# Causal masks written by VectorE, one conversion tile cleared once, and a new fixed order

## The chip, the cores and the metric

One core of a Trainium2 chip. The time is that of one execution on the device, in microseconds; the kernel before has a median of 922.75 us in three runs (922.51 to 926.28). Engines: PE (TensorE: matmuls, into PSUM), DVE (VectorE), ACT (ScalarE), POOL (GpSimd), SP (SyncE, which only issues DMAs).

## The reference

q, k and v are float32 of shape (4, 8, 576, 64): 4 batches, 8 heads, 576 positions. A causal mask in blocks of 64 positions, a softmax, the product with v; the heads are put together to 2304 tokens of 512 features. Two feed-forward layers follow, each 512 to 2048 to 512.

```python
scores = scale * np.matmul(q, k.transpose(0, 1, 3, 2))
mask = block_i >= block_j                  # blocks of 64 positions
scores = np.where(mask, scores, -1000000000.0)
attn = softmax(scores)                     # maximum subtracted, sum + 1e-9
x = concat_heads(np.matmul(attn, v))       # (2304, 512)
h = x @ w_in1;  x = (h * np.tanh(softplus(h))) @ w_out1
h = np.maximum(x @ w_in2, 0.0);  out = (h * h) @ w_out2
```

## The kernel before, in words

**Tokens and passes.** The 2304 tokens are six chunks of 384. Chunks 0 and 1 hold the first 192 positions of the batches ("low" tiles), chunks 2 to 5 the other 384 positions ("high" tiles). A pass is one layer on one chunk: sixteen column blocks f; for each, a first product into `hp` (twelve float16 matmuls of 384 columns, L1206), an activation on ACT (L1212), a split of its result into two float16 parts (ACT, DVE or POOL, L1034 to L1036, and DVE, L744), and a second product into four accumulators `acc` (twelve matmuls, L1272). The first pass (layer 0, chunk 0) runs in float32 instead (L1226, L1231, L1241).

**Attention.** One attention unit is two heads of one batch. A low unit (`attention_lo`) computes its scores by float32 matmuls (L967), row maxima on DVE (L972, L973), the maxima times minus the scale (L974, DVE, SBUF to SBUF), exponentials on ACT (L977), sums and reciprocals on DVE (L980, L982), the scaling of the tiles (ACT L749 or DVE L751), transposes on PE (L990 to L993), a copy (L720 or L722), and the product with v (L1005, L1006). Eight low units of chunk 0 come first, since the first pass needs their result `xs`. A high unit (`attention_hi`) has three score groups of six matmuls (`scores`, L833; 320, 128 and 448 columns, and one more of 448 that needs no mask), then maxima (L843), exponentials (L851), probabilities in two float16 parts (L870, L744), transposes by DMA, and the product with v (L931).

**The mask.** The last 64 key columns of a group are forbidden to the upper 64 query rows. PE adds to them: `above` (ones in its first 64 columns) times `never` (minus 1e24), one matmul for each head (L836) behind the group's six; in a low unit one matmul of 128 columns (L968). Sixteen low units have one, sixteen high units three pairs.

**Weights.** Each weight unit (a megabyte, `decode`) is loaded as raw words (L1053), and a float32 tile is put together from two pieces: POOL clears the tile (L1058), ACT or DVE converts the upper halves into it (the rebias, L1060 or L1061), and DVE shifts the lower bits and ORs them in, in place (the combine, L1062). Layer 0 has sixteen units, each with a tile of its own (parts of `first`, `late` and `ws`); layer 1 has sixteen that share three tiles `wf`. Sums of squares (L1074) and a split into float16 parts follow.

**What sets the order.** The program is a list of 4491 tasks with an engine each. A compressed string, `PLAN`, holds the order of all of them, and the engine of each task that could run on more than one (`planned`). Each engine executes its own tasks in that order and waits at semaphores. The costs given with the tasks and `Sched.opened` serve the search that once made the string; with a string there they change nothing. Tiles of one ring (`R[...]`) are used in turn, and a task waits for the last users of its buffer. `spare["ab"]` is the pair of PSUM banks that all high units share.

Of the kernel before, what the change touches and what calls it, by code (L numbers as in the profile page):

```python
# [59 lines left out]
def seg_len(tiles):  # L60
# [30 lines left out]
    "c-p<02iR4`)wZA6=ST+uAt0hC#b5^uDk7kWD9r*Wh*UuZL2M|ZkzzqbDRyiSMPh=8B?5|K7b&8E(yR2|+Y4vbfA97}Os+rX`>rq7;q0^b>@_p1&GW3qJKUKa"  # L91
    "t?)a>9kil4#T};ucDg=t<u$^cqO2~|POIT|SR-w>?N-)pv*K!j%w}uj_Sr`3pgp$UcH0IU>DF3lRhGA{R#RJSzvWqB9jDG(X!YD4TZ7bU3$#<e+FV;{&aGgr"
    "<F(O#K(?^<*;-p*CEadYW%KM;bDD!x9p|l>R@y9UuJu+(g^(+&pG~fm=Cj(5I#EkmXN&cAhioAl71C))errdmjCR{+`pI@$NlmdIZJRB(GgK7WMK;wk`UZ_Y"
    "v`^XRD>UC`Uz)cS_L*(6ndn|b<u%>@tTk3ZbJ1x8*PMNUmyETR*l2BFuSMv*7~8V=VU-P5sPzt{R@gFRwy@Fxdkd)zwiiDwuyuTP+SAC)Mt+;UjJLL8-7@=&"
    "O-K9tG!5Agxm#mhbtj%a+jZ6*MBy==>Dp@v(l@Fbzc=95%~(84*YR1;>MeDz*0SzwyIogd&n&x63y{m%ExHyRe&+XE{P=)=;rb;}_`>R_DIWTaPa}P5pV|!T"
    "u20Zpwq2=-_Mp0Gw=U6lcxVScJYQc~d!484MBo#m`MGV@?K+v6r)#oR(KUL{s%w>&=p){BP!;u7Ro;w8i&J%`PEi|8vR-=I%BvM4Z`mwOWlj~1w-fcX#@TCp"
    "#@gq2;Y7V+BW#R)rE(h03eVUZcB=|&6u%?+JZ;nTx(z0C8WNG0?Q)Gk>Y)AA>T0wO+OyV5AL~sstF7VIOmA2{;=NT*G4dL@{DeKDK<o69J!(TVOb_G1Yw`1N"
    "yMP=UY7dfq9jq^rc+&bHz17ONXY`oeZGF&uJ=c|1%uUl`yNw;rCr`doA8TX3*nQT;YN(UVCjy`7NBahUPt-njw>kEA{XqPBX$Eh)*fn;&-qEqvgX>&tV&xdW"
    "1^;za8?xprS5nLLwJk-<Z_T^Qu)Yad+SIN@_r^BSE+pQKY^WA!tb5-Y*i*VvAKL?(t*3OcjkCAy2|Ym;g&sd&-SJ07eArhf@ca-tQjz#n)Q5QQOlI~`S-pTC"
    "Khzj9t~2vS+gR6v+3%=_dg?_h$om(pmhN>A+s)+qaO;mXrSuTzYJ_gq4DGj5_&#f$bgvC@gKU6R)(|~nZ@D(?`X^#`9n#mk3VPBWu!g!zFS-U=VP(|Q8Z)OZ"  # L100
    "T0F$HnJxo+ZnF*ev=iRFTr;gJ8P$c;c7u9x5>L~`dQ)|fX`x&3#I+i%Zni=_>=yeYS$4ASwkdX&KC`c_E#FggBRN@JpIZwn@9Jn4C$6QP<SroJk9TiaW9zA_"
    "@oiD;YJ!b7U~OrgqoZ`Wovjk&d2vnvej@j-vI6dMJkSb+Y-}G{Rn@mjD(9ZH%gC~eK#!{6S|ioAlfcxqc8*=hsjrBq-T)KoXuWEYGexoVOpxac^6P9nNA=05"
    "3%Fly!$6jEts2>UHt2T{oZDwaj#Uc~!77ZL#A;3*t)v}qd#sclvUcESo|WcX){0qE@TfSR>R|<~h&3bMZ?z1bX%6l^u2C9920y0Pu&zC5yU7M{;`+18RIWdf"
    "y)Tg^Ly61tdK$bK72!%PGOaRqcj^&*Jq3(@p6t1sTzix(ooEk(>|e0zW9p}J_PEB{Kv1VI(*3}pLgd*P*AL`)n#_8N43qBHaI~3bgRtmneQ%HIkbi@_nbuDu"
    "ZJ&Qg53$d8_NE5vIla!)cy{PQPETR|r@-4@>^+7oAFlh|?fSc|@Q-lc6`dFP3E<Z|Amkj*`$?e8mC-8w(D@$SX`?{8ndHq|@X2=`D~QNsPRC%RALN{W=3lkW"
    "`jgt}eQdgi`2%#5TDhU%S0C`9r|u*3o&d3XlKXw_N!_XnWO`#_{JcG)$MN_vWNK-!x+hq9vTjg6B66#H&Ta;q?jVx~Sre=ZXI(|^4gzJ)RTFiEUz+P4aOpM;"
    "09hM=#O*krO<|(CoQuBJ%Ia}KPK1e@AeZB$Gz04|hY7obGfi}<&bNl_KhG}Xlx*XSbO5t{BJ*yr_MGr8WWi<NdVAH<N;04Z*>tw9hEdVP8nA9FID9s`S63Cg"
    "S{K2yGsxlFh*cfcgPR)aHFCWMd~l&12mUrf>X1G|zN9WB7eCVkES^L5ovgE2v4pnTBvs}7O|$z|ll`jW`%5?x@4`f<V)rRl*^bv6c;f&uD@m50t_oI(yg3Wx"
    "D9yWqb_s|*7DTSDqO5QXnQ;)bE<tqvY)6sx#gN=ZwDLf-N0^_rET{8*6*dRY--&MCU!cukp;?~yeAjVuc5=RUlXv@VmoEyJHPd!q3ic_Wtvt`S_CC<_w#(N0"
    "@o4d`wZW&-O>U*_17RC!s<m}**&^SZ{C`kiz)&q+F=A0bvwcC%OIEY|`5<RUcOEFe24))%_Yb9l%ENcdt-cG{zph(?rWbQvXeF3E5)>=W?ls&TYKCjnfZxm9"  # L110
# [90 lines left out]
class Sched:  # L201
# [76 lines left out]
    def opened(self, t, name):  # L278

        others = [o for o in ("PE", "ACT", "DVE") if o != name]  # L280
        return max((self.shut[b, o] + self.SEM[o][name] for b in t.banks for o in others if (b, o) in self.shut), default=0.0)
# [274 lines left out]
def c_mm16(n):  # L556
    return 2.5 + n / 2.4
# [1038 lines left out]
```

## Time and profile before

| | |
|---|---|
| median of 3 runs | 922.75 us |
| the profiled execution | 925.42 us |
| its span, first to last instruction | 923.6 us |
| PE busy | 895.7 us (97%) |
| DVE busy | 575.5 us (62%) |
| ACT busy | 575.1 us (62%) |
| POOL busy | 63.6 us (7%) |
| mean granted clock of PE | 0.992 |

Busy time is the time in which at least one instruction of the engine is under way. The span is what the trace shows; the execution's own time has a little around it. A wait of PE costs time as long as PE is the engine that ends last; idle time elsewhere need not.

### The profile page before, as it was taken

The numbers are of one execution on the slowest core, as the hardware profiler recorded it, in microseconds if no ns is written. First come the engines' busy times: TensorE is split into PE (matmuls) and PEld (weight loads), VectorE is DVE, ScalarE is ACT, GpSimd is POOL, SyncE is SP. The second block draws the span as 40 slices with busy tenths as digits, with TensorE's granted clock in tenths as the row PEclk, the third lists the DMA queues.
The fourth block names the chain that finished last, engine by engine and source line by source line (L and its number), as shares of the span: only waits on it lengthen the run. The fifth ranks groups of instructions, "written<-read, shape, count | busy, mean of one in ns | idle before, by whom it ended". The sixth has DMA issues, their size and how long they took to land. (4 is left out here: it accounts for less than half of the span.)

```text
span 923.6 us, 15581 instructions
## 1 busy us (share of the span) xinstructions
PE 895.7 (97%) x5786; PEld 533.2 (58%) x5786; DVE 575.5 (62%) x1432; ACT 575.1 (62%) x1121; POOL 63.6 (7%) x86
## 2 busy tenths in 40 slices
PE   4999999999999999999999999999999999999997
PEld 4666555555555555555566555555666666666664
DVE  6668999999989877586721686976531341331211
ACT  3988899999977655447322786987642333544442
POOL 6000201121211100010000000000000000000000
PEclk8899999999999999999999999999999999999999
DMA  7597556999688899738732388696732222343530
GB/s 272 205 362 288 176 159 156 310 291 290 248 299 198 263 231 234 223 107 199 245 98 83 108 224 211 180 241 160 161 101 70 69 69 69 115 137 137 171 114 35
DMA packets 141772, 168.79 MB, mean 183 GB/s; under 512 B 105856, under 2 KB 110976, under 8 KB 141696
## 3 DMA queue, kind: packets, MB, share of 16 engines
q1 hardware_dynamic: 141696, 167.79, 61.2%
q8 instruction: 45, 0.74, 0.3%
q14 instruction: 31, 0.25, 0.1%
HBM read 125.30 MB, written 17.30 MB: 154 GB/s over the span
## 5 line engine op out<-in xcount | busy, mean ns | idle before, releaser
L744 DVE SCALAR_TENSOR_TENSOR g<-h,cst,g 128x384 f16<-128x384 f32 x176 | 108.7, 619 | 222.4 <-ACT g L1034 218.1
L1212 ACT ACTIVATE h<-hp,cst 128x384 f32<-128x384 f32 x176 | 101.3, 577 | 216.9 <-PE hp L1206 205.7
L1272 PE MATMUL acc<-g,ws 128*128 128x384 f16 x1128 | 228.2, 326 | 0.0
L1272 PE MATMUL acc<-g,raw 128*128 128x384 f16 x984 | 205.2, 326 | 1.6 <-ACT ev L1285 1.6
L1206 PE MATMUL hp<-x,first 128*128 128x384 f16 x768 | 154.8, 326 | 1.0 <-ACT h L1212 0.9
L1272 PEld LDWEIGHTS <-ws 128*128 128x128 f16 x1128 | 108.7, 98 | 72.8 <-issue 2.2
L1272 PEld LDWEIGHTS <-raw 128*128 128x128 f16 x984 | 95.3, 98 | 65.5 <-issue 3.3
L1206 PEld LDWEIGHTS <-first 128*128 128x128 f16 x960 | 92.4, 98 | 63.8 <-issue 3.9
L1206 PE MATMUL hp<-x,raw 128*128 128x384 f16 x552 | 117.9, 326 | 0.0
L1034 ACT ACTIVATE g<-h,cst 128x384 f16<-128x384 f32 x119 | 72.8, 613 | 27.8 <-PE acc L1272 25.6
L1206 PEld LDWEIGHTS <-raw 128*128 128x128 f16 x648 | 61.6, 98 | 40.8 <-issue 1.9
L1206 PE MATMUL hp<-x,ws 128*128 128x384 f16 x408 | 84.7, 326 | 0.4 <-DMA ws<-wspill 0.4
L744 DVE SCALAR_TENSOR_TENSOR pb<-pad,st,pb 128x384 f16<-128x384 f32 (+2 forms) x96 | 71.1, 750 | 13.9 <-ACT pb L870 13.9
L870 ACT ACTIVATE pb<-pad,st 128x384 f16<-128x384 f32 (+2 forms) x96 | 66.4, 713 | 21.3 <-DVE st L863 6.4
L851 ACT ACTIVATE pad<-spare,st,sq 128x448 f32<-128x448 f32 (+1 forms) x96 | 65.1, 680 | 9.8 <-DVE st L846 4.7
L1206 PEld LDWEIGHTS <-ws 128*128 128x128 f16 x504 | 47.8, 98 | 30.8 <-DMA ws<-wspill 0.5
L843 DVE TENSOR_REDUCE st<-spare 128x2 f32<-128x896 f32 (+1 forms) x48 | 47.8, 996 | 10.3 <-PE spare L836 7.6
L1226 PE MATMUL hp<-xs,first 128*128 128x384 f32 x128 | 47.5, 491 | 0.0
L1206 PE MATMUL hp<-late,first 128*128 128x384 f16 x192 | 41.5, 326 | 0.0
L833 PE MATMUL spare<-q 64*128 64x448 f16 (+2 forms) x384 | 38.5, 306 | 1.5 <-ACT pad L851 1.1
L1217 ACT ACTIVATE h<-h 128x384 f32<-128x384 f32 x75 | 38.4, 514 | 0.6
L1241 PE MATMUL acc<-h,late 128*128 128x384 f32 x96 | 36.9, 495 | 0.2 <-ACT h L1231 0.2
(238 smaller groups left out, 1122.9 us busy)
## 6 DMA issues: line engine op xcount, KB each, us to landing
ws<-wspill SPq DMA_DIRECT2D x68, 512.0 KB, 4.6
raw<-wspill SPq DMA_DIRECT2D x68, 512.0 KB, 4.1
raw<-in_w_dram SPq DMA_DIRECT2D x27, 1023.8 KB, 6.5
wspill<-wn SPq DMA_DIRECT2D x24, 512.0 KB, 3.9
qk<-in_qp_dram SPq DMA_DIRECT2D x16, 480.0 KB, 4.6
vs<-in_va_dram SPq DMA_DIRECT2D x16, 320.0 KB, 4.1
pad<-in_w_dram SPq DMA_DIRECT2D x5, 1023.8 KB, 6.8
out_dram<-ev SPq DMA_DIRECT2D x24, 192.0 KB, 2.4
```

What stands on the lines that cost most here:

```text
L744: return sch.add("DVE", c_dve(n) + 62 * ap, lambda: nc.vector.scalar_tensor_tensor(dst(), a(), s() if ap else s, c(), op0, op1), r=r, w=w, ...
L833: nc.tensor.matmul(out=pp.t[:, hd, o:o + k1 - k0], lhsT=qh.t[rows, u, a:a + 128], rhs=qh.t[rows, w, nq + k0:nq + k1], start=p == 0, stop=p ...
L843: sch.add("DVE", c_dve(2 * (o1 - o0)), lambda: nc.vector.reduce_max(both(st, j, r0), pp.t[r0:, :, o0:o1], axis=AX.X), w=[(pp, 0), (st, j)])
L851: t = sch.add("ACT", c_act(o1 - o0, True, 3), lambda hd=hd: nc.scalar.activation(pf[hd].t[r0:, k0:k0 + o1 - o0], pp.t[r0:, hd, o0:o1], AF. ...
L870: sch.add("ACT", c_act(n, False, 1), lambda pb=pb, pv=pv, s=s: nc.scalar.activation(pb.t[:, 0:i + 1, 0, :], pv(), AF.Copy, scale=s()), r=[ ...
L1034: "ACT": ("ACT", c_act(n, False, 1), lambda: nc.scalar.activation(dst(0), src(), AF.Copy, scale=s()), False),
L1206: nc.tensor.matmul(out=hp.t[:, 0:n], lhsT=w.t[:, f % 2, a, 128 * k:128 * k + 128], rhs=x.t[:, c, k, 0:n], start=k == 0 and i == 0, stop=k ...
L1212: sch.add("ACT", c_act(n, True, 1), lambda: nc.scalar.activation(h.t[:, 0:n], hp.t[:, 0:n], (AF.Mish, AF.Relu)[l], scale=hs()), r=[(cst, ( ...
L1217: "ACT": ("ACT", c_act(n), lambda: nc.scalar.activation(hv(), hv(), AF.Square), False),
L1226: nc.tensor.matmul(out=hp.t[:, 0:n], lhsT=wf.t[:, 512 * (f % 2) + 128 * k:512 * (f % 2) + 128 * k + 128], rhs=xs.t[:, k, 0:n], start=k == ...
L1241: ts.append(sch.add("PE", c_mm(4 * n), lambda m=m, acc=acc: nc.tensor.matmul(out=acc.t[:, 0:n], lhsT=wf.t[:, 512 * (f % 2) + 128 * m:512 * ...
L1272: nc.tensor.matmul(out=acc.t[:, 0:n], lhsT=wo.t[:, f % 2, a, 128 * m:128 * m + 128], rhs=g.t[:, c, 0:n], start=f == 0 and i == 0, stop=f = ...
```

## The change

Four things. The mask matmuls are gone, and DVE writes a large negative number into the forbidden part of the scores, in PSUM, between the matmuls and the row maximum. For layer 0 the rebias goes into one separate tile `top`, cleared once in the prologue, whose low halves stay zero; the combine reads it and writes the weight tile, so the sixteen clears on POOL are dropped. Layer 1 is as before. The ring `us` has eight buffers instead of six. The order string is new; costs and `opened` are those with which it was searched.

```diff
-    R["us"] = sb("us", [128, 2 * NGRP], F32, 6)
+    R["us"] = sb("us", [128, 2 * NGRP], F32, 8)
...
+    top = pad.bitcast(F32)[:, 2048:3072]
+    R["top"] = fixed([top])
...
     make_identity(nc, ident)
+    nc.gpsimd.memset(top, 0.0)
...
-    above = cp.tile([128, 128], BF16, name="above")
-    nc.vector.memset(above[:, 0:64], 1.0)
-    nc.vector.memset(above[:, 64:128], 0.0)
-    never = cp.tile([128, 2], BF16, name="never")
-    nc.vector.memset(never, -1e24)
...
-            for i in R["raw"].insts:
+            for i in R["raw"].insts + R["top"].insts:
...
-                                         start=p == 0, stop=p == 2 and not mask)
-                for hd in range(2 if mask else 0):
-                    nc.tensor.matmul(out=pp.t[:, hd, o + k1 - k0 - 64:o + k1 - k0], lhsT=above, rhs=never[:, 0:1].to_broadcast([128, 64]), start=False, stop=True)
+                                         start=p == 0, stop=p == 2)
...
+            sch.add("DVE", 110.0, lambda pp=pp, n=n: nc.vector.memset(pp.t[0:64, :, n - 64:n], -1e25), w=[(pp, 0)])
             peak(st, 0, pp, 0, 0, n)
             if i == 2:
+                sch.add("DVE", 110.0, lambda pp=pp, n=n: nc.vector.memset(pp.t[0:64, :, n + 64:n + 128], -1e25), w=[(pp, 0)])
                 sch.add("DVE", c_dve(256), lambda pp=pp, n=n: nc.vector.tensor_copy(tail.t, pp.t[:, :, n:n + 128]), w=[(pp, 0), tail])
...
-                nc.tensor.matmul(out=pp.t[:, o:o + m], lhsT=qs.t[:, q:q + 128], rhs=qs.t[:, k:k + m], start=o == 0, stop=False)
-            nc.tensor.matmul(out=pp.t[:, 128:256], lhsT=above, rhs=never[:, 0:1].to_broadcast([128, 128]), start=False, stop=True)
+                nc.tensor.matmul(out=pp.t[:, o:o + m], lhsT=qs.t[:, q:q + 128], rhs=qs.t[:, k:k + m], start=True, stop=True)
...
+        sch.add("DVE", 135.0, lambda: nc.vector.memset(pp.t[0:64, 128:256], -1e9 / scale), w=[pp])
...
-        high = lambda: wf.t.bitcast(F16).rearrange("p (c two) -> p c two", two=2)[:, :, 1]
-        sch.add("POOL", 1000.0, lambda: nc.gpsimd.memset(wf.t, 0.0), w=[wf])
+        top = wf if l else R["top"].new()
+        high = lambda: top.t.bitcast(F16).rearrange("p (c two) -> p c two", two=2)[:, :, 1]
+        if l:
+            sch.add("POOL", 1000.0, lambda: nc.gpsimd.memset(wf.t, 0.0), w=[wf])
...
-            U(wf.t), mids(), 13, U(wf.t), ALU.logical_shift_right, ALU.bitwise_or), r=[raw], w=[wf], lock=True)
+            U(wf.t), mids(), 13, U(top.t), ALU.logical_shift_right, ALU.bitwise_or), r=[raw, top], w=[wf], lock=True)
```

The order strings can be decoded: three bytes a task, two for its number and one for its engine. Before: PE 1738 tasks, DVE 1426, ACT 871, POOL 80, SP 376. After: PE 1738, DVE 1523, ACT 848, POOL 54, SP 376. Ahead of the first matmul of the first pass stand 57 ACT, 76 DVE and 19 POOL tasks before, and 49, 95 and 7 after.

## Rows read from the trace of the kernel before

**Rows 1.** The page's busy table: engine, busy us, share, instructions.
```profile
span 923.6 us, 15581 instructions
PE 895.7 (97%) x5786; PEld 533.2 (58%) x5786; DVE 575.5 (62%) x1432; ACT 575.1 (62%) x1121; POOL 63.6 (7%) x86
```
**Rows 2.** Busy time by stretch: length, then each engine's busy us and instructions.
```profile
core 0: us, PE busy (x) PEld busy (x) DVE busy (x) ACT busy (x) POOL busy (x), PEclk, DMA share, GB/s
0.00:23.00 23.00, 10.80 (x52) 10.22 (x54) 14.15 (x34) 7.01 (x26) 14.44 (x25) 0.83 0.75 274
23.00:46.00 23.00, 21.93 (x134) 15.91 (x135) 15.99 (x55) 21.14 (x68) 0.00 (x0) 0.87 0.58 203
23.00:92.00 69.00, 67.66 (x325) 44.67 (x326) 50.75 (x142) 60.36 (x152) 0.64 (x2) 0.96 0.76 284
92.00:277.00 185.00, 181.01 (x1133) 103.03 (x1132) 175.32 (x425) 171.47 (x278) 31.57 (x39) 1.00 0.79 241
139.00:462.00 323.00, 314.21 (x2197) 182.58 (x2196) 274.39 (x693) 232.40 (x418) 37.79 (x47) 1.00 0.83 235
```
**Rows 3.** PE's waits: who, for whom, us in total, times, longest.
```profile
PE acc L990 <- ACT pt L749: 8.2, 1, 8.2
PE acc L967 <- DMA qk<-in_qk_dram: 4.0, 1, 4.0
...
PE acc L1272 <- ACT ev L1285: 1.6, 1, 1.6
```
**Rows 4.** Order of time at the start: start, us, what; idle before it in brackets.
```profile
2.10 0.23 POOL L962 MEMSET pt<- 128x64 f32 x2
2.26 1.84 POOL L1058 MEMSET late<- 128x1024 f32 x2
...
6.80 8.22 DVE L974 TENSOR_SCALAR st<-st 128x3 f32<-128x3 f32 x1
...
14.05 0.95 POOL L1058 MEMSET first<- 128x1024 f32 x1
15.12 0.42 ACT L977 ACTIVATE pt<-acc,st 128x192 f32<-128x192 f32 x1 [13.11 <-DVE st L973]
...
19.35 0.45 PE L990 MATMUL acc<-ident,pt 128*128 128x128 f32 x1 [8.23 <-ACT pt L749]
```
**Rows 5.** Order of time on PE: two score groups, and the first pass's first matmuls.
```profile
9.98 1.08 PE L967 MATMUL hp<-vs 128*128 128x192 f32 x6
...
20.23 1.81 PE L967 MATMUL acc<-vs 128*128 128x192 f32 x6
...
41.72 1.51 PE L1226 MATMUL hp<-xs,first 128*128 128x384 f32 x4
```
**Rows 6.** Groups by line and shape: count, busy us, mean ns of one, idle before.
```profile
L973 DVE TENSOR_REDUCE st<-spare 128x1 f32<-128x64 f32 x8 | 1.7, 216 | 0.0
L889 DVE COPY tl<-spare 128x256 f32<-128x256 f32 x16 | 7.3, 458 | 0.0
L749 ACT ACTIVATE pt<-pt,st 128x192 f32<-128x192 f32 x14 | 6.4, 456 | 0.3 <-DVE st L982 0.3
L720 ACT ACTIVATE pt<-spare 128x448 f32<-128x448 f32 x5 | 2.7, 535 | 0.1
L1074 ACT ACTIVATE wsq<-first 128x1024 bf16<-128x1024 f32 x8 | 8.4, 1055 | 0.1
```
**Rows 7.** The same view: rebias on ACT and combine on DVE.
```profile
L1060 ACT ACTIVATE first<-raw 128x1024 f16<-128x1024 bf16 x2 | 2.7, 1352 | 0.0
L1062 DVE SCALAR_TENSOR_TENSOR late<-raw,late 128x1024 uint32<-128x1024 uint32 x4 | 4.8, 1212 | 2.6 <-ACT late L1060 2.6
```
**Rows 8.** PE around masked and unmasked scores; all mask matmuls; those of 92:277.
```profile
580.56 0.74 PE L833 MATMUL spare<-q 64*128 64x448 f16 x6
581.23 0.23 PE L836 MATMUL spare<-never,above 128*128 128x64 bf16 x2
581.31 0.65 PE L1206 MATMUL hp<-x,raw 128*128 128x384 f16 x3
...
586.76 0.74 PE L833 MATMUL spare<-q 64*128 64x448 f16 x6
587.44 0.66 PE L1206 MATMUL hp<-x,raw 128*128 128x384 f16 x3
...
L836 PE MATMUL spare<-never,above x96: 195/199/204, 100.7 to 645.1; 128*128 128x64 bf16 x96
...
92.00:277.00 185.00, 3.98 (x34) 1.93 (x34) 1.00 0.79 241
```

More of the change, by code (lines that the diff above doesn't have):

```diff
@@ L95 @@
[L95 to L110, printed above, removed]
@@ new lines @@
+    "Chj^;g|rwh>ui^m(E`qP&>Y*wxeXHMeu3Xn`jNZWTLTr)UMs12_J=L7-=NxI3y}4Av?{2AnuetLwGBS|t+wWJa<a`wGUJ|~x$mHzs1^1jXE)e1tE_zb2OJh!"
+    "8o5qEf?rMAY(+K0cG^ZH+iy$lE#+XHidg11TMM6Gt*}<XajU(f!pQdwr#9L?%NJT@fqjcqJJEC}@{K{3KhboBy{#=aom0!uW`ylU*XOxokIlECddFs=?|JT4"
+    "PH(qd>#w`yu;VD@+CcTuM$QjcZ{+K(wdmIa-p{Ce=%a4PvdspeRbSR~?GClmqiEMfw_@+L?9a8|t(|7uW%?BxthTE)(|)p5)(R_6x7*+~6;EA-<-bFge%h(#"
+    "P;Q4}u3e<9oNlhc@SbH`@JKyuvrZfFM>S2i_Nu9>@Htm++dcZ$u2pp`em=5Q)l{pY`Rb}A_Je(BpIdeOI+;lO7)fX7YdcdDu<AG)&+8hUq%Z6XdjtR6Xs=;`"
@@ new lines @@
+    "PwZ8^`m%kY5A0*TZ!Pt_mD79nti5eV>j%AQAL?DbVH1g$CVGvCDxg>FCG6fnAK}j;dI74-l+v^Iyq>XfXh8&NwC%T%x=4>h^SJ%W+Aa1neyQMw>mj0N7&n}!"
+    "-B_Y2_MNAD@%Sj4jrW#esYmU0-C=92up5q_9<saaCiS<WczT)j<JAXm+(tZA(O~OspX*M$(<T#tAL|;shMhS!UdwEp%BdsKv&i04J1Dzohk6rdz0u-VY}B07"
+    "KUx7S-j$!PsHR<^C-t*Efli||Ti&k5|2g)E##>9Q{5cu+mR)9Z^}ZXbGq6%Uov$JK8tYEi1$GWzx}Q@g=`-^8Y*o>#HW&+**8nYX7wH9J;xsi<8{HOIPgm(F"
+    "yIeQuMPl!9;<OnNakRRr7d|)}NfzVPQDne8tl1e0714|CQ5$Z<bg~{)U)M<$u;pXAl2~j<)IMbQal<7lr5~|gOO??uTWJHaTU)n`obHRp^>wQ~?QQ~9TIeRC"
@@ new lines @@
+    "{6_1k0ahR1cG0!m+TR+X(^TuBn_1my*K?waYGdJvwp6|B1a!QOJgTl9))XC^sssA=u={nTYozk}l6#8k3M;D<Tw|R}6wbHK#ARL;*Rg71b=2NnVs(k`Qg9k="
+    "jfv^vpxL=<VO@#p=dGTNwe#!~HMbhp#6BXTyQ{U%#1eJcOS#G*M_tRH@o=#3eB$P8GW<l{Z|8uF)vYFISX5`RSBLy8t?ITxwZXB0b}AmaKsD?!kmY7LW~`c>"
+    "2;Sw@QE0Z;jt8$QsiYl?MmuaU(Onr#>Ht0!0j~<+iMH0-3J|?TtswZ++VX>8>xsbD_NDS#%G!cm<CG$1-_b$e$-FJM3&51u^bi^^0>2h=PfL(s2pZqZs}|8U"
+    "(?;t)tpq2>fUJWwTDRkw5#Z5}<iKOBouFrlkx?2BzL(Q5Vs|9b{;(b<w}<EvR_@V4(50-FLO+xooo{!;a{w_q7Y?_8RWpd)Cp8crd;G)jd{D0|xcg840{Hea"
@@ new lines @@
+    "aeOy^zejKCd%QUq-#5@V<nG;?WOwQ<&~zBo?^#Wv{RwWq)3wtge>ai%A+nCtotovZ0Z~7;nSLNSb&D>BXCu(!2Opr;4PZfkJw_Z&vRCW@BE78}Z7&kFJ=~+}"
+    "Ne0|NjE@0HAENg41dq<(zGsl~G3%$N@K}9444U4ge&pftdXDqYA=P!D!{=%S|6go?>kI0ww;|-g_4xTzRdSEusYbe-__@JGlKGdw^$NAOT5vlE9zP5g^(XpU"
+    "k^@)T17Ku3yB(~rOsq6fd$2yAy90cy3Ep0cr*E~3(c=nYb+y&D0oE84SwR#xR0-V#`ZPwq3w0Se(-1r)hN;6NLEwhE+}7|Z(4+&lIfL8V<E_QyRSi{ub7i<*"
+    "q~ob%vyiwUQF^|9BC-p+(qv2%xSmh#C=R06ux8}XDx&>s;^7CK%IV5*Iav?Dp}I{Z;;Y%o+;TEf*Px>3CpV9?^5pGVR)N?%iSGtFoT2ho9IU)l6+zQutP<GO"
@@ L170 @@
+    "n{9Lsqf4s%p$RA2kI!dkm87kVH`0+i4&$E1kN>!q{{lD@{gU8FAE}``l+rGVqj+*iLQ98fn825gz?8oy%YSOe#XV^Zr*VbP#^?X1B>!aNUp{A@saQ;MDg9r{"
+    "3^wi"
 )
@@ L278, in opened @@
     def opened(self, t, name):
-        others = [o for o in ("PE", "ACT", "DVE") if o != name]
+        others = ("ACT", "DVE") if name == "PE" else ("PE",)
         return max((self.shut[b, o] + self.SEM[o][name] for b in t.banks for o in others if (b, o) in self.shut), default=0.0)
@@ L823, in scale_of, with scores @@
                     [qs, (sq, 2), (qh, (0, j))], [(qh, (1, j))], 1)
-        def scores(i, pp, o, k0, k1, mask=True):
+        def scores(i, pp, o, k0, k1):
             a = tile_q(i)[0] - q0
@@ L833, in mm @@
                         nc.tensor.matmul(out=pp.t[:, hd, o:o + k1 - k0], lhsT=qh.t[rows, u, a:a + 128], rhs=qh.t[rows, w, nq + k0:nq + k1],
-                                         start=p == 0, stop=p == 2 and not mask)
-                for hd in range(2 if mask else 0):
-                    nc.tensor.matmul(out=pp.t[:, hd, o + k1 - k0 - 64:o + k1 - k0], lhsT=above, rhs=never[:, 0:1].to_broadcast([128, 64]), start=False, stop=True)
-            steps.append(sch.add("PE", 3 * (c_mm16(k1 - k0) + 16) + (110.0 if mask else 0.0), mm, r=[(qh, (p, j)) for p in range(2) for j in range(2)], w=[(pp, 0)]))
+                                         start=p == 0, stop=p == 2)
+            steps.append(sch.add("PE", 3 * (c_mm16(k1 - k0) + 16), mm, r=[(qh, (p, j)) for p in range(2) for j in range(2)], w=[(pp, 0)]))
         both = lambda st, j, r0=0: st.t[r0:, 2 * j:2 * j + 2]
@@ L894, in attention_hi @@
         pp, pf = R["ab"].new(), [R["pf", 4].new() for _ in range(2)]
-        scores(4, pp, 0, 0, 448, False)
+        scores(4, pp, 0, 0, 448)
         peak(last, 0, pp, 0, 0, 448)
@@ L1056, in decode @@
         mids = lambda: raw.t.bitcast(U32).rearrange("p (c two) -> p c two", two=2)[:, :, 0]
-        high = lambda: wf.t.bitcast(F16).rearrange("p (c two) -> p c two", two=2)[:, :, 1]
-        sch.add("POOL", 1000.0, lambda: nc.gpsimd.memset(wf.t, 0.0), w=[wf])
+        top = wf if l else R["top"].new()
+        high = lambda: top.t.bitcast(F16).rearrange("p (c two) -> p c two", two=2)[:, :, 1]
+        if l:
+            sch.add("POOL", 1000.0, lambda: nc.gpsimd.memset(wf.t, 0.0), w=[wf])
         choose(ENG["rebias"], {
-            "ACT": ("ACT", c_act(n) + 90.0, lambda: nc.scalar.activation(high(), ends(), AF.Copy), False),
-            "DVE": ("DVE", c_dve(n), lambda: nc.vector.tensor_copy(high(), ends()), True)}, [raw], [wf])
+            "ACT": ("ACT", 1330.0, lambda: nc.scalar.activation(high(), ends(), AF.Copy), False),
+            "DVE": ("DVE", 746.0, lambda: nc.vector.tensor_copy(high(), ends()), True)}, [raw], [top])
         sch.add("DVE", c_dve(n), lambda: nc.vector.scalar_tensor_tensor(
-            U(wf.t), mids(), 13, U(wf.t), ALU.logical_shift_right, ALU.bitwise_or), r=[raw], w=[wf], lock=True)
+            U(wf.t), mids(), 13, U(top.t), ALU.logical_shift_right, ALU.bitwise_or), r=[raw, top], w=[wf], lock=True)
         sch.group = None
```

127 lines of the change are left out of this document (63 added, 64 removed).

## The prediction, on record before the result

> **What bounds the kernel now.** I read the busy table first. PE is busy 895.7 us of a 923.6 us span [rows 1]. A kernel with PE at 97% can gain in two ways only: less work on PE, or fewer of its 27.9 us of idle time. The second view, the busy time by stretch, says where that idle time lies: 12.2 us in the first 23 us, 1.1 us from there to 46, and 8.8 us between 139 and 462; the rest is mostly the draining of the last tiles [rows 2]. The third view, PE's waits by the one waited for, names the largest single one: 8.2 us, once, for a scaled softmax tile of the first attention unit. The next is 4.0 us for the first load; no other single wait is above 1.6 us [rows 3].
>
> The fourth view is the order of time at the start, and it holds the point of this case [rows 4]. DVE's multiply of L974, on three columns, starts at 6.80 us and ends at 15.02. GpSimd clears weight tiles back to back, at about 0.92 us each; the last of fifteen clears starts at 14.05, takes 0.95 and ends at 15.00. The multiply, whose operands lie in SBUF, ended 0.02 us later. ACT's first exponential followed at 15.12, after 13.11 us of waiting, and PE's first transpose at 19.35, after 8.23 us. So clears that nobody needs so early hold up a tiny instruction, and three engines behind it.
>
> The Trainium skill (SBUF — State Buffer, section Who interferes with whom) says that DVE in a two-port mode and GpSimd take their shared port exclusively, for one whole instruction. By its words the multiply would wait for one clear, at most 0.95 us; the row shows 8.2 us, across nine of them. The row decides: a queue of clears keeps the port.
>
> **The change, part by part.**
>
> *Clears.* The sixteen clears of layer 0 go; one of the same size (the separate tile) comes in the prologue. The new order string, decoded, still puts three clears, for layer 1, and four small ones at the front of GpSimd's queue. Before, GpSimd had three big clears, the identity and two small ones behind it at 4.1 us [rows 4]; one more big one (0.92) and two small ones (0.23 together) end at 5.3 us. The first multiply is due at 6.8 plus the mask write ahead of it, so it finds the port free with 1.5 us in hand. The chain then moves from 15.02 to about 7.0: 8.2 us earlier, less 0.25 for that write (priced below), plus some 0.1 for the mask matmul that no longer ends the scores. I book -8.0 us.
>
> What is late next? ACT: it is busy 21.1 us of 23 between 23 and 46 us [rows 2], and the first matmul of the first layer starts only at 41.72 [rows 5]. In the decoded strings ACT has 57 tasks ahead of that matmul before and 49 after. It loses six scalings of 192 columns (0.46 each) and three copies (at most 0.54 each), and gains one sum of squares (1.06): between -1.7 and -3.3, so about -2.5 us on ACT [rows 6]. DVE takes most of these and ten mask writes; it was busy 16 of 23 us there. PE limits the rest: it was busy 21.9 of 23 us, with a clock granted at 0.87 there against 1.00 later [rows 2]. Six score matmuls took 1.08 us at 9.98 and 1.81 at 20.23 [rows 5], the upper and the lower of its levels of 2.4 and 1.2 GHz, and between them PE stood still for 8 us. Without that pause it may stay up. So this second gain lies between 0 (PE as slow as before) and 4 us (ACT's 2.5, the 1.1 us of idle time, and the handovers between them); I take -1.5.
>
> The weights must come as much earlier. Their loads are paced by buffers that become free with the conversions, and these stand in the same queues of ACT and DVE as the chain, so they shift with it; DMA was busy 0.75 and 0.58 of the first two stretches [rows 2]. I cost it at nothing.
>
> *Single conversion tile.* Each rebias of layer 0 must now wait for the combine before it. One pair takes 1.35 us on ACT and 1.21 on DVE [rows 7]; sixteen in series are 41 us of the 69 between 23 and 92 [rows 2]. In the new order the first combine stands ahead of the next rebias; where that holds the wait is nothing. I take 0; the other end, 1.2 us (a whole combine) for each of fifteen, is a rival below.
>
> *Masks off PE.* A 448-column score group with mask took from 580.56 to 581.31, the same without from 586.76 to 587.44: 0.75 against 0.68 us, so 0.07 for two mask matmuls, a pair. There are 96 of them, 48 pairs [rows 8]: 3.4 us, and PE is busy 98% of the stage where they begin [rows 2]. For the low tiles it is one matmul each, between half a pair and a pair, 0.05; ten of the sixteen stand ahead of the first layer, where the chain and not PE decides, so six count: 0.3 us. Together -3.7.
>
> *Masks onto DVE.* 48 writes of 2x64 columns and 16 of 128, on 64 rows. The trace has none. The nearest rows are DVE on PSUM: 64 columns in 0.216 us, 256 in 0.458 [rows 6]. Their line gives 0.30 for 128 columns, the end above; its value at no column, 0.135, is the end below. I take 0.25, nearer the upper end, because those are operations on PSUM of this very size. That is 16 us on DVE in all, 9 to 19 by the ends. DVE has idle time enough over the whole span, so what counts is the stage from 92 to 277, where it is busy 175.3 of 185 us and ACT 171.5 [rows 2]. There 34 of the mask matmuls ran [rows 8], so 17 writes or 4.3 us; 9.7 us are free. Behind a write that waits for PE stand the row maximum, the scales and, by way of ACT, the transposes, while PE has other matmuls queued; only where its order holds the next score group does it wait. I book +0.4, from -3 (the new order closes a third of the small waits of 139 to 462 us) to +8 (rival B).
>
> *New order.* By the decoded strings the skeleton is the same: each attention unit stands beside the same matmuls as before within a few dozen of them, and the last third of PE's order hardly differs. DVE gets 97 tasks more: the 64 writes, and 33 that were ACT's or GpSimd's. ACT has 23 fewer, GpSimd 26, sixteen of them clears. I count no gain for it beyond the parts above.
>
> Sum: -8.0 - 1.5 - 3.7 + 0.4 = -12.8 us. The profiled execution took 925.42 us, 1.8 more than its span, and 2.7 more than the median of the three runs, 922.75; the difference is carried over to that: 909.9 us.
>
> **Rivals.**
>
> A, *the middle closes too*. With GpSimd freer and ACT relieved, the small waits of 139 to 462 us go as well. For: none is above 1.6 us [rows 3], and the engines they end on have 8 us more. Against: in an order fixed beforehand a wait that goes leaves another one. It would take 6 to 8 us more: 902 to 904.
>
> B, *given back in the saturated stage*. If ACT and DVE, at 93 and 95% between 92 and 277 us [rows 2], and not PE set the pace there, PE comes 10 us earlier and waits. Seventeen writes fall there; at 0.25 us each and as much again for one more handover between engines (a guess; the trace shows none) they lengthen chains by 17 x 0.5 = 8 us. Against: DVE and ACT were both held up at the start and gain the 8 us themselves. Time: 922.75 - 12.8 + 8 = 917.9.
>
> C, *only one clear is waited for*. If the port were given up after each clear, the multiply would have ended by 7.7 us, and the 8.2 us would have another cause that stays: 922.75 - 4.8 = 917.9 again. The 15.00 beside 15.02 speaks against it [rows 4]. It is what the rule quoted above from the Trainium skill (SBUF — State Buffer, Who interferes with whom) would make of this start.
>
> D, *slower: the single conversion tile stalls ACT*. Its place is 23 to 92 us, with ACT idle 8.6 us of 69 [rows 2]. If a rebias reaches the head of ACT's queue while the combine before it stands behind other work on DVE, exponentials and the activation after it wait, and PE with them. Fifteen waits of w cost 15w - 8.6; from w = 1.4 us the 12.8 us are gone, from 1.75 the kernel is slower by over 0.5%. One wait between these two was 2.6 us before, the other way round [rows 7]; w = 2.6 gives 30 us and 940. The new order's first combines stand early, so this is unlikely.
>
> **How the numbers follow.** Forecast 0.67, with its own range of 905 to 914 (second gain 0 to 4 us, writes by both ends, middle -3 to +2); A 0.12; B 0.12; C 0.04; D 0.05. Predicted: 909.9 us. From 903 to 918 lie the forecast, half of A, B and C, some 0.85 in all. About 0.5%, or 4.6 us, is what can be told from no change: under 918.1 is faster, which holds for the forecast, A and most of B and C, and over 927.4 is slower. Faster 0.93, the same 0.04, slower 0.03.
>
> **What would show it.** Right: L974's first multiply at some 0.2 us, ACT's first exponential near 7 us, PE's first transpose near 11, the first layer's first matmul at 30 to 34 instead of 41.7, nothing between a score group and the next matmul, DVE writes of 0.14 to 0.30 us, and PE's busy time down by some 4 us or more. Wrong: the multiply still waiting at the start, PE idle by more than 15 us between 92 and 323 us, or rebiases on ACT that wait for DVE between 30 and 90 us.

## The result, and the profile after

The changed kernel took 914.94 us (914.31 to 914.98; a fourth execution of 5238 us is left out), against 922.87 us (922.51 to 926.28) for the kernel before on the same chip: a ratio of 0.9904, 95% interval 0.9874 to 0.9933. It lies 5 us above the predicted 909.9, just above the forecast's own range of 905 to 914, and inside the 903 to 918 that take in the rivals. The experiments ran on three chips, called A, B and C here, and the gain is not the same on them (after_again, before_again and before_third_look are the two kernels, unaltered, measured once more):

| kernel | chip | median us (lowest to highest, executions) | ratio to before on that chip, 95% |
|---|---|---|---|
| before | A | 923.14 (918.18 to 930.61, 17) | |
| before | B | 915.14 (911.73 to 926.26, 35) | |
| before | C | 915.48 (913.32 to 923.56, 29) | |
| after_again | C | 915.30 (912.27 to 920.97, 12) | 1.0003 [0.9980, 1.0027] |
| before_again | C | 915.17 (913.46 to 922.88, 12) | 0.9986 [0.9955, 1.0017] |
| before_third_look | A | 924.37 (921.64 to 927.53, 12) | 1.0007 [0.9990, 1.0024] |

On chip C the change gained nothing. The times of the kernel before in the first measurement are like those on A.

The profiled execution of the kernel after took 914.98 us. Its busy table and PE's longest waits answer to [rows 1] and [rows 3]:

```profile
span 913.1 us, 15430 instructions
PE 888.1 (97%) x5674; PEld 527.6 (58%) x5674; DVE 585.3 (64%) x1526; ACT 567.4 (62%) x1096; POOL 43.6 (5%) x61
```

```profile
PE acc L966 <- DMA qk<-in_qk_dram: 4.0, 1, 4.0
PE hp L1207 <- DVE x L743: 1.7, 2, 1.0
PE spare L966 <- DMA vs<-in_qk_dram: 1.5, 2, 0.8
PE hp L1207 <- ACT h L1213: 1.3, 1, 1.3
PE acc L1273 <- ACT ev L1286: 1.3, 1, 1.3
PE spare L930 <- DMA late<-pb: 1.2, 1, 1.2
```

PE's busy time fell by 7.6 us and its idle time by 2.9, and the 8.2 us wait is gone. The matmuls of the start took longer before, at a lower clock (1.81 us against 1.08 for the same six in [rows 5]), so not all of the 7.6 us is mask work. The busy time by stretch, to be held against [rows 2], shows where:

```profile
0.00:23.00 23.00, 17.48 (x108) 15.29 (x108) 14.53 (x71) 14.86 (x59) 4.62 (x14) 1.00 0.90 316
23.00:46.00 23.00, 22.07 (x115) 14.02 (x114) 18.49 (x56) 20.39 (x48) 0.00 (x0) 1.00 0.95 358
23.00:92.00 69.00, 68.07 (x313) 42.07 (x312) 60.03 (x158) 58.15 (x122) 0.00 (x0) 1.00 0.78 294
92.00:277.00 185.00, 180.08 (x1117) 103.33 (x1117) 177.30 (x441) 173.43 (x281) 29.64 (x35) 1.00 0.85 250
139.00:462.00 323.00, 313.58 (x2151) 182.68 (x2149) 269.99 (x707) 220.52 (x390) 35.33 (x43) 1.00 0.81 227
554.00:646.00 92.00, 88.64 (x637) 49.61 (x637) 67.71 (x172) 70.34 (x154) 1.90 (x2) 1.00 0.78 191
```

In the first 46 us PE is granted its full clock (1.00, where it was 0.83 and 0.87 before) and has 5.5 us idle in the first 23 instead of 12.2. The new loss is late: 3.4 us idle from 554 to 646. The start, to be held against [rows 4] and [rows 5], in the order of time of each engine:

```profile
4.94 0.24 POOL L961 MEMSET pt<- 128x64 f32 x2
...
6.04 0.17 DVE L970 MEMSET acc<- 64x128 f32 x1 [4.90 <-PE acc L966]
6.96 0.17 DVE L973 TENSOR_SCALAR st<-st 128x3 f32<-128x3 f32 x1
...
7.23 0.42 ACT L976 ACTIVATE pt<-acc,st 128x192 f32<-128x192 f32 x1 [5.21 <-DVE st L973]
...
11.62 0.30 PE L989 MATMUL acc<-ident,pt 128*128 128x128 f32 x1
...
30.41 0.81 PE L1227 MATMUL hp<-xs,first 128*128 128x384 f32 x2
```

GpSimd is done by 5.2 us, the multiply takes 0.17 us instead of 8.22, PE's first transpose starts at 11.6 instead of 19.4, and the first layer at 30.4 instead of 41.7.

### The profile page after: what moved, and what is told of

Its sections match the earlier page's. It is cut to its first block, busy times and chain, and to the rows that moved or that the text cites. A ratio compares the mean times of both kernels' runs of the same rounds, so it can differ in the third digit from the quotient of the medians.

```text
span 913.1 us, 15430 instructions
## 1 busy us (share of the span) xinstructions
PE 888.1 (97%) x5674; PEld 527.6 (58%) x5674; DVE 585.3 (64%) x1526; ACT 567.4 (62%) x1096; POOL 43.6 (5%) x61
## 5 line engine op out<-in xcount | busy, mean ns | idle before, releaser
L1207 PE MATMUL hp<-x,first 128*128 128x384 f16 x768 | 157.2, 326 | 2.3 <-DVE x L743 1.7
L1033 ACT ACTIVATE g<-h,cst 128x384 f16<-128x384 f32 x113 | 69.2, 613 | 16.6 <-PE acc L1273 16.2
L1218 ACT ACTIVATE h<-h 128x384 f32<-128x384 f32 x68 | 34.9, 513 | 0.7
```

The source lines that it names most:

```text
L1033: "ACT": ("ACT", c_act(n, False, 1), lambda: nc.scalar.activation(dst(0), src(), AF.Copy, scale=s()), False),
L1207: nc.tensor.matmul(out=hp.t[:, 0:n], lhsT=w.t[:, f % 2, a, 128 * k:128 * k + 128], rhs=x.t[:, c, k, 0:n], start=k == 0 and i == 0, stop=k ...
L1218: "ACT": ("ACT", c_act(n), lambda: nc.scalar.activation(hv(), hv(), AF.Square), False),
```

## The experiments

**One part at a time, chip A.** Four kernels took the change apart: the clears removed (with the single conversion tile), the masks moved, both, each in the old order; and the new order with the masks left on PE. The old order's string was kept but for tasks that had to move behind what they depend on.

```
clears_only      - sch.add("POOL", 1000.0, lambda: nc.gpsimd.memset(wf.t, 0.0), w=[wf])      (layer 0)
                 + top = wf if l else R["top"].new()
masks_only       - nc.tensor.matmul(... lhsT=above, rhs=never ...)
                 + sch.add("DVE", 110.0, lambda: nc.vector.memset(pp.t[0:64, :, n - 64:n], -1e25), ...)
both_old_order     both of these, PLAN of the kernel before
new_order_masks_on_pe   the kernel after, without the edit of masks_only
```

> The kernel before with its own order, the separate conversion tile and without the sixteen clears of layer 0; masks stay on PE (eleven conversion tasks stand a little later, where the single tile asks for it). Theory T, the clears are the gain and the rest about cancels: the first multiply takes 0.2 us at about 7 us, the first layer's first matmul starts near 33.5 (41.7 less 8.2), and the time is 913.5 to 916. Rival O, the new order is needed to keep the gain: the start is as early, but 3 us or more are given back later, 917.5 to 920.

> The kernel before with its own order and its clears, masks written by DVE just ahead of each row maximum. As the prediction summed it (-3.7 on PE, +0.4 for waits): 919 to 920. Rival M, the writes lengthen the chains of the high units and PE waits for what it has saved: 922 to 925, PE busy down by 3.7 us and its idle time up by as much or more.

> Clears and masks as in the kernel after, but in the order of the kernel before. Theory T as predicted: -8.2 - 3.7 + 0.4, about 911 to 912, so that the new order is worth nothing or less. Rival M: 915 to 917, since the masks bring nothing. Rival O: 917 or more, and the new order is worth 2 us or more.

> The kernel after with its order and its clears gone, but the masks added by PE as before and the 64 writes left out of DVE's order. By the prediction's sum 914.9 + 3.3 = 918. Rival M: 913 to 915.5, because the waits of PE between 462 and 646 us (4.0 us after, 0.4 before) go with the writes.

Measured, with the ratio to before: clears_only 926.19 us (1.0023 [1.0005, 1.0041]); masks_only 933.52 (1.0109 [1.0078, 1.0141]); both_old_order 936.36 (1.0137 [1.0108, 1.0167]); new_order_masks_on_pe 911.93 (0.9873 [0.9846, 0.9901]). In the old order each part alone made the kernel slower, and missed both of its expected ranges; both together fit rival O alone (917 or more). new_order_masks_on_pe came out below what either theory said. The new order is worth 14.3 us where the clears are gone (926.19 - 911.93). And masks moved to DVE cost time in both orders: 10.4 us in the old one (933.52 - 923.14), 3.0 in the new one (914.94 - 911.93, the former in the first measurement).

In clears_only the start gained its 8 us and lost them again. Two rows of DVE, two of ACT and one of PE, in order of time, and two stretches of the same kernel:

```profile
89.10 1.21 DVE L1062 SCALAR_TENSOR_TENSOR ws<-raw,pad 128x1024 uint32<-128x1024 uint32 x1
...
90.34 1.34 ACT L1060 ACTIVATE pad<-pad 128x1024 f16<-128x1024 bf16 x1
92.98 1.06 ACT L1074 ACTIVATE wsq<-first 128x1024 bf16<-128x1024 f32 x1 [1.29 <-DVE first L1062]
...
94.18 0.16 PE L1077 MATMUL spare<-us,onesq 128*128 128x4 bf16 x1 [4.46 <-ACT wsq L1074]
...
97.77 1.23 DVE L1062 SCALAR_TENSOR_TENSOR ws<-raw,pad 128x1024 uint32<-128x1024 uint32 x1 [4.83 <-ACT pad L1060]
```

```profile
23.00:46.00 23.00, 20.69 (x94) 13.07 (x95) 13.81 (x35) 17.88 (x46) 0.00 (x0) 0.85 0.75 274
92.00:139.00 47.00, 44.66 (x175) 23.95 (x175) 40.45 (x99) 40.52 (x66) 3.95 (x4) 0.93 0.47 144
```

"pad" holds the single conversion tile. The rebias at 90.34 starts as the combine of 89.10 ends, so it waited for the tile. Behind it ACT's sum of squares waits for a combine, PE 4.5 us for that sum, and a later combine 4.8 us for its rebias. PE is idle for 2.3 us in each of the two stretches, and its clock is granted at 0.93 in the second, where [rows 2] has 1.00. It is rival D's mechanism, in an order that had sixteen tiles to convert into.

**Is it the single tile or the order? Chip B.** clears_only with four conversion tiles:

```
-    R["top"] = fixed([top])
+    tops = [top] + [wft[:, 1024 * i:1024 * i + 1024] for i in range(NWF)]
+    R["top"] = fixed(tops)
```

> The old order with the sixteen early clears gone, as in clears_only (926.2 us, where the gain of the start was lost again between 64 and 97 us), but with four conversion tiles used in turn in place of one: the separate tile and the three weight tiles of layer 1, which are free until then. Only 2 tasks of the old order must be delayed, against 11 with a single tile. Theory S (the single tile ate the gain: a rebias waits for the combine before it, and ACT's and DVE's queues stand behind it): the 8 us stay, 914 to 917 us, and PE's wait of 4.5 us for the sum of squares at 94 us is gone. Rival O (an order made for the late start gives the time back whatever the tiles do): 921 to 926 us, with other waits in the same stretch.

Measured: 913.96 us (911.45 to 915.40), 0.9978 [0.9958, 0.9999] of before on that chip. That is theory S: 12 us less than with one tile and the eleven tasks that it delays (on another chip), and the wait for the sum of squares is gone. But the kernel before takes only 915.14 there, so on chip B the clears were worth 1 us, not 8. A later kernel on that chip suggests why.

**Masks left out altogether, chip B.** This kernel and the next leave out the masking, so that scores above the diagonal count.

```
new_order_no_masks   - sch.add("DVE", 110.0, ... memset(pp.t[0:64, ...], -1e25) ...)   (all 64, in the kernel after)
old_order_no_masks   - nc.tensor.matmul(... lhsT=above, rhs=never ...)                 (all 112, in the kernel before)
new_order_low_masks_on_dve   the kernel after, its 48 writes for high tiles put back as matmuls
```

> The changed kernel with its 64 mask writes on DVE left out and nothing in their place, so the scores above the diagonal are not masked; all else is in the order of the changed kernel. With the same order, masks on PE gave 911.9 us and masks on DVE 914.9. Theory H2 (the 3.4 us of mask matmuls are a real gain for PE, and the writes cost more than that in waits): 908 to 909.5 us, so that the writes alone cost about 6 us. Rival H1 (PE's 3.4 us are worth nothing, because the chains through DVE and ACT set the pace where the masks are): 911.5 to 912.5 us, and the writes cost 3.

> The kernel before with its mask matmuls left out and no writes in their place (scores above the diagonal not masked), the sixteen clears and the order as before. H2 (PE's mask time counts): 919 to 920.5 us, so that the writes in masks_only (933.5) cost 13 us. H1 (it doesn't count): 922.5 to 923.5, and the writes cost 10. A time above 924.5 would mean that already the shorter PE blocks upset the old order, and that the writes are not the whole cause of masks_only.

> The changed kernel with the 16 masks of the low tiles written by DVE, as in it, and the 48 of the high tiles added by PE, as before. The losses of the changed kernel were read at 462 to 646 us, in the high units. If the high units carry the cost: 911 to 912 us, no more than with all masks on PE (911.9). If the low units, which lie in the start and the saturated stage 92 to 277 us, carry it: 914 to 915.

Measured: new_order_no_masks 914.48 us (0.9970 [0.9939, 1.0002]); old_order_no_masks 916.79 (1.0017 [0.9994, 1.0041]); new_order_low_masks_on_dve 912.14 (0.9959 [0.9938, 0.9980]). H2 is out: without any mask the new order is not at 908 to 909.5. In medians it is 2.3 us slower without masks than with the high ones on PE (914.48 and 912.14, same chip), but the difference goes largely with the clock. Six of the 12 executions without masks had a mean clock under 0.999, two of the 12 with the high ones on PE; at 0.999 or more the averages are 912.7 and 912.2, which is within the noise. So taking the mask matmuls from PE gains nothing, as H1 says; that it costs something by itself is not shown. At the same clock the changed kernel averages 914.1 (chip C) and 914.7 us (first measurement), so the writes cost some 1.4 to 2.0 us, across chips. The cost goes with the high tiles: with these left on PE the time is 912.14, as with all of them there (911.93). In the old order the 1.7 us more without masks are within the noise; the times expected for that kernel started from 923 and did not fit this chip.

The start of old_order_no_masks, with all sixteen clears still in it, was the surprise (DVE's rows, then GpSimd's):

```profile
6.53 0.29 DVE L966 TENSOR_SCALAR st<-st 128x3 f32<-128x3 f32 x1
...
9.76 0.88 DVE L966 TENSOR_SCALAR st<-st 128x3 f32<-128x3 f32 x1
...
11.73 0.30 PE L982 MATMUL acc<-ident,pt 128*128 128x128 f32 x1 [1.10 <-DVE pt L746]
...
5.84 0.95 POOL L1050 MEMSET late<- 128x1024 f32 x1
6.74 0.97 POOL L1050 MEMSET first<- 128x1024 f32 x1
7.66 0.95 POOL L1050 MEMSET late<- 128x1024 f32 x1
...
9.66 3.82 POOL L1050 MEMSET first<- 128x1024 f32 x4
...
14.34 1.06 POOL L1050 MEMSET first<- 128x1024 f32 x1
```

GpSimd clears back to back until 15.4 us, as in [rows 4]. But the first multiply ends at 6.82, as the clear of 5.84 to 6.79 does, and a later one, from 9.76, takes no more than one clear, 0.88 us. PE transposes at 11.7 us.

**Is the wait in every execution? Chips C and A.** The two kernels unaltered, and the kernel after with eleven useless clears put back at the front of GpSimd's queue:

```
-   sch.add("POOL", 1000.0, lambda: nc.gpsimd.memset(wf.t, 0.0), w=[wf])
+   sch.add("POOL", 1000.0, lambda: [nc.gpsimd.memset(wf.t, 0.0) for _ in range(12 if (k, j) == (0, 1) else 1)], w=[wf])
```

> The kernel before, unaltered, with a profile of its own beside its times. In the job of clears_only it took 923.1 us, in the job of clears_only_four_tiles, on another chip, 915.1 (911.7 to 926.3); and a kernel that still has all clears (old_order_no_masks) showed there a first multiply of 0.29 us instead of 8.2. Theory P: the long wait behind GpSimd's clears is not in every execution; it depends on the chip and the execution which engine gets the port when a clear ends. Then the profile shows either a multiply of over 6 us, a granted clock near 0.83 in the first 23 us and a time of 921 or more, or a multiply of at most 1.2 us, a clock near 1.00 and 911 to 917. Rival K: chips differ in the clock alone; then the multiply takes 8 us in the profile also where the time is 911 to 917.

> The changed kernel, unaltered, on the same chip as before_again. Theory P: it has no long clears that could be waited for, so it takes 914 to 915.5 us on any chip, and is worth 8 us against a kernel before that waits, and nothing (within 2 us) against one that doesn't. Rival K: it gains about as much on every chip, so 907 to 908 where the kernel before takes 915.

> The changed kernel with eleven further clears of 1024 columns put back at the front of GpSimd's queue (one weight tile of layer 1 is cleared twelve times in place of once), so that GpSimd clears back to back until about 15 us as before; nothing else needs them. Where the kernel before shows the long wait: the first multiply ends at about 15 us again, the first matmul of the first layer comes some 8 us later, and the time is 920 to 923 (theory: the clears' absence is the gain of the change) or 914 to 917 (rival: in the new order the start is hidden behind something else). Where the kernel before doesn't show it: 914 to 916 by both.

> The kernel before, unaltered, once more, for a profile of one of its faster executions. Theory P (the wait behind the clears is in some executions and not in others, and it, with the lower clock behind it, is what separates 921 from 914): a profiled execution of 911 to 917 us shows a first multiply of at most 1.2 us, PE's first transpose before 13 us, the first matmul of the first layer near 33 in place of 41.7 and a clock near 1.00 in the first 46 us; one of 920 or more shows 8.2 us again. Rival K: an execution of 911 to 917 us shows the 8.2 us too, and makes up for it elsewhere.

before_again took 915.17 us in the median, but its profiled execution took 922.88, and it shows the long wait (order of time, and the first stretch, PE's clock granted at 0.80):

```profile
6.74 0.95 POOL L1058 MEMSET first<- 128x1024 f32 x1
6.81 8.23 DVE L974 TENSOR_SCALAR st<-st 128x3 f32<-128x3 f32 x1
...
14.07 0.95 POOL L1058 MEMSET first<- 128x1024 f32 x1
```

```profile
0.00:23.00 23.00, 10.18 (x52) 9.53 (x52) 14.14 (x33) 7.02 (x26) 14.46 (x25) 0.80 0.74 274
```

before_third_look ran on chip A, where all its executions took over 921 us, and its profile shows the wait again (first row); so does that of masks_only, of the same chip (second row):

```profile
6.85 8.18 DVE L974 TENSOR_SCALAR st<-st 128x3 f32<-128x3 f32 x1
```

```profile
6.70 8.32 DVE L970 TENSOR_SCALAR st<-st 128x3 f32<-128x3 f32 x1
```

new_order_clears_back took 918.58 us (1.0026 [0.9999, 1.0053]) on chip C; its profiled execution, of 916.68 us, did not wait long (DVE's rows, then GpSimd's):

```profile
6.83 0.39 DVE L968 TENSOR_SCALAR st<-st 128x3 f32<-128x3 f32 x1
...
8.53 0.71 DVE L968 TENSOR_SCALAR st<-st 128x3 f32<-128x3 f32 x1
...
15.37 0.96 DVE L968 TENSOR_SCALAR st<-st 128x3 f32<-128x3 f32 x1
...
3.33 12.96 POOL L1054 MEMSET wf<- 128x1024 f32 x13
```

So behind such a queue of clears a profile shows either the long wait (four profiles: the kernel before three times, masks_only once) or waits of at most one clear (two profiles, of other kernels). Where in a clear the multiply starts does not tell them apart: 0.07 us after the start of one (6.81 and 6.74) it waited for nine, 0.10 us after (9.76 and 9.66, old_order_no_masks) for one. For the kernel before, 45 of 46 executions on chip A took over 918.2 us, on B 5 of 35, on C 9 of 41. A time above 918.2 does not prove the wait, though: after_again, which has no such queue, took 918.8 to 921.0 us in 3 of its 12 executions on C, at mean clocks of 0.993 to 0.998. Theory P's time for the kernel after on chip C holds (914 to 915.5), and rival K's 907 to 908 doesn't. For the clears put back, both theories said 914 to 916 without the long wait; the median is 3.3 us above that of after_again, and the profile has the first layer's first matmul at 32.0 us, where after_again has 30.6. So waits of up to one clear each cost something too.

What is not shown: no profile of the kernel before in one of its faster executions was obtained. That these are the ones without the long wait is inferred, from old_order_no_masks, from clears_only_four_tiles (which has no such queue of clears and takes 914.0, about the time of the faster executions), and from the granted clock: in 50 executions of before on B and C at a mean clock of 0.999 or more the mean time is 914.4 to 914.9 in each of three sets of runs, and no execution on A has such a clock. On C the kernel after at that clock takes 914.1 (7 executions).

## Why the prediction came out as it did

**Clears, -8.0, and the second gain, -1.5: right, for an execution that waits.** All that should show it did: multiply, exponential, transposes, clock, first matmul at 30.4. That the first measurement met a chip on which nearly every execution takes the longer time is luck: on C the same two kernels differ by 0.1 us. The trace followed through to the end confirms that the lead is kept. The table gives the time at which so many us of the weight matmuls (the lines of the two layers' two products) were done, summed from their busy time in steps of 4 us; the second row is the difference to the first, and minus is earlier:

```
bulk work done       48     144     289     385     530     674     915 us
before_third_look    97.3   198.0   348.0   440.2   562.0   694.2   876.8
four tiles          -10.6   -10.0    -9.7   -10.6   -10.6   -10.2   -10.3
```

Ten us at the first layer, ten at the end. In medians it is 8.9 (922.87 to 913.96, across chips). Read wrongly was how firm [rows 4] are: one profiled execution was taken for every execution. Rival C, by which only one clear is waited for, was given 0.04; judged by their times, it is what most executions on B and C do, and there the start has nothing to give. The Trainium skill (SBUF — State Buffer, section Who interferes with whom) has the shared port held for one whole instruction; the 0.88 us of old_order_no_masks agrees, the 8.18 to 8.32 us of the four profiles above don't.

**Single tile, 0: right in the new order only, and not for the reason given.** "Where that holds the wait is nothing" does not cover all of it. One of the signs of being wrong that the prediction named did show: twice between 30 and 90 us a rebias on ACT waits for DVE's combine.

```profile
33.67 1.36 ACT L1061 ACTIVATE pad<-raw 128x1024 f16<-128x1024 bf16 x1 [1.29 <-DVE late L1063]
...
67.68 1.35 ACT L1061 ACTIVATE pad<-raw 128x1024 f16<-128x1024 bf16 x1 [3.78 <-DVE first L1063]
```

Nothing of it reaches PE, which has no idle time at all from 46 to 92 us. In the old order the tile costs 12 us, across chips.

**New order, 0: wrong.** "I count no gain for it beyond the parts above" fails. It carries the single tile, and beyond that it is worth about 2 us: 913.96 with four tiles in the old order (chip B), 911.93 with one in the new (chip A).

**Masks, -3.7 and +0.4: this is the step that failed.** They measure +3.0. The failing sentence is "3.4 us, and PE is busy 98% of the stage where they begin": it takes a busy share for a bound. DVE's writes took 0.165 us each, under the 0.25 assumed (first row: those of the high tiles). PE's busy time in the new order is 890.2 us with the masks on PE (second row; span 909.7) and 888.1 without: 2.1 us less, not 3.7. In the old order the difference is 4.4 (891.7 with four tiles, 887.3 in old_order_no_masks), so the price lies between.

```profile
L884 DVE MEMSET spare<- 64x128 f32 x32 | 5.3, 165 | 6.8 <-PE spare L832 5.8 <-PE spare L1148 0.2
```

```profile
PE 890.2 (98%) x5786; PEld 530.2 (58%) x5786; DVE 575.0 (63%) x1465; ACT 567.2 (62%) x1096; POOL 43.4 (5%) x61
```

But the time saved on PE does not stay saved: its idle time is 25.0 us in the changed kernel and 19.5 with the masks on PE. The same table against the new order with masks on PE; minus is earlier, and "after" is the profile of the first measurement:

```
bulk work done              48     145     290     387     532     677     918 us
new_order_masks_on_pe       85.8   187.3   333.9   425.8   550.3   683.2   866.4
after                       -0.4    -2.2    -1.1    +0.5    +0.2    +2.8    +2.8
after_again                 -0.1    -2.1    -1.0    +0.2    -0.2    +1.2    +1.2
new_order_low_masks_on_dve  -0.7    -2.1    -2.4    -2.0    -0.4    +0.9    +0.9
new_order_no_masks          +2.0    +0.5    +0.7    +2.6    +2.2    +3.0    +3.0
```

The changed kernel is 2.1 us ahead at 187 us, and gives it back, and more, between 290 and 680 us. With the low masks on DVE and the high ones on PE the profile gives back 3.0 us too and ends 0.3 us before after_again; that the high tiles carry the cost rests on the medians. The 2.0 us by which the kernel without masks is late at the start are another matter. There PE waits 3.05 us for a load of vs (0.8 at most in the changed kernel), and the six score matmuls behind the pause take 1.97 us where six before it took 1.04; the clock of the first 23 us is 0.93:

```profile
10.05 1.04 PE L957 MATMUL acc<-vs 128*128 128x192 f32 x6
...
14.58 1.97 PE L957 MATMUL spare<-vs 128*128 128x192 f32 x6 [3.05 <-DMA vs<-in_qk_dram]
```

In one place the wait that takes the saving can be named. It lies in the old order, where old_order_no_masks is 0.3 us ahead of four tiles at 339 us and 4.3 behind at 553 (same chip). ACT's copy of an output tile without masks (first row), and the same copy with masks and four tiles (second row):

```profile
448.25 0.58 ACT L1277 ACTIVATE ev<-acc,cst 128x384 f32<-128x384 f32 x1 [7.39 <-DMA out_dram<-ev]
```

```profile
444.69 0.58 ACT L1287 ACTIVATE ev<-acc,cst 128x384 f32<-128x384 f32 x1 [5.47 <-DMA out_dram<-ev]
```

The output tiles share two buffers, and an earlier store must land first. SP issued the stores of this stretch behind five loads of weights; they took 6.3 us to land, in the other kernel 4.5 (medians of two). PE then waits 3.25 us for ACT here, and 1.33 there. The sums of PE's waits in the two kernels without mask matmuls, masks_only and old_order_no_masks, name the same pair:

```profile
PE acc L1268 <- ACT ev L1281: 4.2, 2, 3.3
PE spare L927 <- DMA late<-pb: 4.1, 4, 1.4
```

```profile
PE acc L1264 <- ACT ev L1277: 4.2, 2, 3.2
PE spare L924 <- DMA late<-pb: 3.9, 3, 2.3
```

In both, the waits go back to a transfer: ACT's copy waits for a store, and PE for the transposed probabilities. In the new order the loss is spread over waits of at most 1.3 us each, for DVE, ACT and DMA. From 277 to 690 us they add up to 8.2 us in the profile of the changed kernel, 6.8 in after_again, 6.5 without masks, 4.9 with the low masks on DVE and 2.5 with all of them on PE, and none of them is for a mask write. Much of it lies in the stretch from 554 to 646 us, where the changed kernel has PE busy for 88.64 us and the one with masks on PE for 91.58:

```profile
554.00:646.00 92.00, 91.58 (x691) 51.97 (x689) 66.68 (x162) 73.17 (x158) 1.90 (x2) 1.00 0.80 196
```

Why the saving is lost is open. With the order of each engine fixed, a wait can grow only where durations differ; which of them do it in the new order was not found. Executions at a mean clock of 0.999 or more average 911.7 us with masks on PE (4 of 6), 912.2 with the low ones on DVE (10 of 12), 912.7 with none (6 of 12) and 914.1 to 914.7 with all on DVE (10 of 15, both measurements). So at that clock the kernel with no masks loses 1.0 us or less, within the noise, and the larger part of the masks' +3.0 comes with the writes, although PE waits for none of them directly.

**The sum.** By terms, in medians and across chips: clears with what follows at the start -8.9 for -9.5; order -2.0 for 0; masks +3.0 for -3.3. Together -7.9 for -12.8. The masks' miss is 6.3 us; the order, booked at nothing, hid 2.0 of it. That the sum still lies between 903 and 918 owes something to that, and to the chip. Rival B named the giving back, but put it in the saturated stage of 92 to 277 us, where PE got only 0.9 us more idle time; rival A's middle stayed as it was (139 to 462 us: 9.4 us idle, 8.8 before).

The best version seen is the new order with the masks left on PE: 911.93 us on chip A, 0.9873 of before; with the low masks on DVE it is 912.14 on chip B, 0.9959.

## What to carry to other kernels

A wait that one profile shows need not be in every execution: profile the kernel twice, better on two chips, before pricing its removal, and look at the spread of its times, which showed here that something comes and goes. A busy share of 98% did not make every microsecond of PE's work worth one of the kernel's; ask of each that is saved which transfer or buffer it will meet, above all in an order that is fixed. And parts of a change that was searched together must not be priced alone: in the old order the same two edits cost 13 us.

## What the runs showed of the hardware that was not expected

A DVE multiply of three columns behind a queue of GpSimd clears of 0.95 us waited 8.18 to 8.23 us in the three profiles of the kernel before, across nine clears, and in the profiles of two other kernels with such a queue its longest took 0.88 and 0.96 us, about one clear. By the times of the kernel before, the long wait is in most executions on one chip (45 of 46 over 918.2 us) and in few on the others (5 of 35 and 9 of 41); that is inferred, not seen, and other executions without such a queue are over 918.2 us too. A DVE write of 64x128 fp32 into the scores took 0.165 us, less than a reduction of 64 columns there (0.21 us).
